# One transposing load for two weights, another order at the head, and a closing loop one tile further ahead

## The chip, the cores and the metric

The kernel runs on one core of a Trainium2 chip. The metric is the device time of one launch in microseconds, shown as the median of several runs. Beside it there is one profiled execution, whose span and trace are read here.

## The reference

Two branches read the same input x (2048 tokens by 512) and are mixed by a gate per token. Branch A is linear attention with a softmax feature map, 32 heads of 16; branch B is a hidden layer of 1376 with ReLU. All inputs and the output are bf16.

```python
g = sigmoid((x * gate_w).sum(-1, keepdims=True))
# branch A
q, k, v = split_heads(x @ wqkv)                       # 32 heads of 16
pq, pk = einsum(q, w_phi), einsum(k, w_phi)           # per head, 16 x 16
phi_q = concat([softmax(pq), softmax(-pq)], -1)       # 32 features
phi_k = concat([softmax(pk), softmax(-pk)], -1)
kv, z = einsum("bhsf,bhsd->bhfd", phi_k, v), phi_k.sum(over s)
o = (phi_q @ kv) / (phi_q @ z + 1e-6)
a = merge_heads(o) @ wo
# branch B
b = relu(x @ w1) @ w2
return g * a + (1 - g) * b
```

## The kernel before

**How an order is written.** The kernel is written out by hand, engine by engine. `p.op(engine, instruction, after=[...], ev=...)` appends one instruction to its engine's list; each engine runs its own list strictly in order, and an instruction waits for the events named in `after`. `p.dma("sp", ...)` does the same for a transfer on SyncE's queue. PSUM has eight banks; `free[bank]` holds the event that releases a bank, set by whatever last evicted it, and the next group of matmuls into that bank waits for it. So what decides when something runs is its place in its engine's list and the bank that it writes.

**The head.** SyncE's queue loads, in this order: half of the first 512 tokens of x (`loadx0`), W1 in row slabs of 128 (`loadw1`, columns 0 to 1023 of each slab; slab 0 in two parts), the other half of the first tokens by a transposing load (`x0t`), slab 3, then columns 1024 to 1375 of all four slabs (`w1r`, line 178), the feature weights, the value weights WV (line 182), the query and the key weights by one transposing load each (`wqk0` and `wqk1`, line 185, 512 x 512), and the other three chunks of x by transposing loads (`x1` to `x3`, line 188). TensorE meanwhile transposes a quarter of x itself, then runs `slab(t)` for t = 0 to 3 (line 520): eight hidden units of the first 512 tokens, each in a bank of its own, one slab of W1 at a time. Two further units follow (`hunit(0, 8)` and `hunit(0, 9)`, line 272).

**The fold.** The feature map is linear up to the softmax, so its weights are folded into the query and key weights: `pre(i)` (line 306) makes one of eight pieces of WQK, 0 to 3 for queries, 4 to 7 for keys, with 4 matmuls of 120 columns each, in banks 0, 1, 6, 7 in turn. A piece is evicted by VectorE (even i, line 311) or ScalarE (odd i, line 313). Before, the order at this place is value tiles 0 and 1, folds 0 to 3, value tile 2, folds 4 to 7, and then `rest(0)` (line 284), the ragged last unit of the hidden layer with the gate's column.

**The passes over 16 tiles of 128 tokens.** In pass m TensorE runs `atile(m)` (line 328, the query and key projections; ScalarE's exponentials of line 348 read them), `kv(m - 3)` (line 426, the running sum over tokens), `vtile(m + 3)` (line 404, the values three tiles ahead, bank 2) and the hidden units that the list `mid[m]` names, each of 4 matmuls of 512 columns. Hidden units take banks 3, 4, 5 in turn (`nextbank`), and so do `rest` and the second of the early value tiles. After the passes come the units in `late`, with the last three `kv` groups between them; `kvfin` on VectorE then turns the sums into KVNZ.

**The closing loop.** For each tile: `nd(m)` (line 458, 8 matmuls, numerator and denominator, banks 0 and 1 or 2 and 3), which VectorE divides (lines 464 and 468) and SyncE transposes into OT by a transfer (line 474); `finB(m)` (line 483, 11 matmuls, the hidden layer's second product) into one of banks 4, 5, 7; `finA(m)` (line 492, 4 matmuls, the attention's output product) into bank 6, which ScalarE scales by the gate into TFA (line 497); and `comb(m)`, VectorE's (1 - g) times finB plus TFA (line 506), which frees finB's bank and is followed by the store (line 511). Before, `finB` runs one tile ahead of `finA`, `nd` three tiles ahead. In pass m it is emitted as

```python
            if m + 1 < NT - 1:
                finB(m + 1, FB[(m + 1) % 3])
```

with `FB = (4, 5, 7)`. `finB` waits for `free[bank]`, and `comb` sets it: `free[bank] = [f"cb{m}{tag}"]`. The last tile is done in two column parts.

Of the kernel before, what the change touches and what calls it, by code (L numbers as in the profile page):

```python
# [68 lines left out]
def bass_gated_mix__linear_kernel_hedgehog__dense_activation_relu__prompt_kernel(  # L69
# [13 lines left out]
    S, D = x2.shape  # L83
    H = A_w_phi.shape[0]
    DH = A_w_phi.shape[1]
    DFF = B_w1.shape[1]
    P = 128
    NT = S // P
    NDT = D // P
# [12 lines left out]
    KU = KT - 1  # L102
    NR = DFF - KU * P

    with ExitStack() as es:
# [55 lines left out]
        def loadw1(t, c0=0, c1=DFF, tag=""):  # L161
            p.dma("sp", lambda e: e.dma_start(  # L162
                out=W1[:, t, c0:c1], in_=B_w1[t * P:(t + 1) * P, c0:c1]), f"w1{t}{tag}", ev=f"w1{t}{tag}")
# [6 lines left out]
        p.early("sp")  # L170
        loadw1(0, 0, 4 * P, "a")
        loadw1(0, 4 * P, 8 * P)
        for t in (1, 2):
            loadw1(t, 0, 8 * P)
        p.dma("sp", lambda e: e.dma_start_transpose(  # L175
            out=XT[:, 2:4, 0:512], in_=x2[0:512, 2 * P:4 * P]), "x0t", ev="x0t")
        loadw1(3, 0, 8 * P)
        p.dma("sp", lambda e: e.dma_start(
            out=W1[:, :, 8 * P:DFF], in_=B_w1[:, 8 * P:DFF].rearrange("(j p) n -> p j n", p=P)), "w1r", ev="w1r")
        p.dma("sp", lambda e: e.dma_start(  # L180
            out=WPS[:, :, :], in_=A_w_phi.rearrange("(g hl) r c -> (hl r) g c", g=NDT)), "wps", ev="wps")
        p.dma("sp", lambda e: e.dma_start(  # L182
            out=WV[:, :, :], in_=A_wqkv[:, 2 * D:3 * D].rearrange("(j p) n -> p j n", p=P)), "wv", ev="wv")
        for i in range(2):
            p.dma("sp", lambda e, i=i: e.dma_start_transpose(  # L185
                out=WQKT[:, 4 * i:4 * i + 4, :], in_=A_wqkv[:, i * D:(i + 1) * D]), f"wqk{i}", ev=f"wqk{i}")
        for c in range(1, NCH):
            p.dma("sp", lambda e, c=c: e.dma_start_transpose(
                out=XT[:, :, c * 512:(c + 1) * 512], in_=x2[c * 512:(c + 1) * 512, :]), f"x{c}", ev=f"x{c}")
# [75 lines left out]
        def nextbank():  # L265
            rot[0] += 1
            return 3 + (rot[0] - 1) % 3
# [32 lines left out]
        def pre(i):  # L300
            which, dt = i // 4, i % 4
            bank = (0, 1, 6, 7)[i % 4]
            dst = WQK[:, which, dt * DE:(dt + 1) * DE]
            after = [f"wqk{which}"] + [f"wbd{g}" for g in range(NDT)] + free[bank]
            for gt in range(NDT):
                p.op("pe", lambda e, gt=gt: e.matmul(  # L306
                    PS[:, bank, gt * 8 * FE:(gt + 1) * 8 * FE], WQKT[:, which * NDT + gt, dt * P:(dt + 1) * P],
                    Wbd[:, gt, :], start=True, stop=True),
                    after=(after if gt == 0 else ()), ev=(f"pm{i}" if gt == NDT - 1 else None))
            if i % 2 == 0:  # L310
                p.op("dve", lambda e: e.tensor_copy(dst, PS[:, bank, 0:DE]), after=[f"pm{i}"], ev=f"pc{i}")
            else:
                p.op("act", lambda e: e.activation(dst, PS[:, bank, 0:DE], ACT.Copy),
                     after=[f"pm{i}"], ev=f"pc{i}")
            free[bank] = [f"pc{i}"]
# [138 lines left out]
        def nd(m):  # L454
            b0 = 2 * (m % 2)
            after = [f"tq{m}", "kvz0"] + free[b0] + free[b0 + 1]
            for g in range(NG):
                p.op("pe", lambda e, g=g: e.matmul(  # L458
                    PS[:, b0 + g // 4, (g % 4) * GW:(g % 4) * GW + 68],
                    PHQ[:, g, m * P:(m + 1) * P], KVNZ[:, g, :], start=True, stop=True),  # L460
                    after=(after if g == 0 else ["kvz1"] if g == 4 else ()), ev=(f"nd{m}" if g == NG - 1 else None))
            r = m % 2
            ob = m % 3
            p.op("dve", lambda e: e.reciprocal(
                RDEN[:, r, :].rearrange("p (g h) -> p g h", g=NG),
                bass.AP(tensor=PS, offset=b0 * 512 + 64, ap=[[EPS, P], [GW, NG], [1, HG]])),
                after=[f"nd{m}"], ev=f"rd{m}")
            p.op("dve", lambda e: e.tensor_tensor(  # L468
                OTM[:, ob, :].rearrange("p (g h d) -> p g h d", g=NG, h=HG),
                bass.AP(tensor=PS, offset=b0 * 512, ap=[[EPS, P], [GW, NG], [DH, HG], [1, DH]]),  # L470
                bass.AP(tensor=RDEN, offset=r * H, ap=[[2 * H, P], [HG, NG], [1, HG], [0, DH]]), ALU.mult),
                after=[f"rd{m}"] + ([f"to{m - 3}"] if m >= 3 else []), ev=f"om{m}")
            free[b0] = free[b0 + 1] = [f"om{m}"]
            p.dma("sp", lambda e: e.dma_start_transpose(
                out=OT[:, :, m * P:(m + 1) * P], in_=OTM[:, ob, :]), f"to{ob}", after=[f"om{m}"], ev=f"to{m}")
# [3 lines left out]
        def finB(m, bank, cs=slice(0, 512), tag=""):  # L479
            n = cs.stop - cs.start  # L480
            for kt in range(KT):
                M = P if kt < KU else NR
                p.op("pe", lambda e, kt=kt, M=M: e.matmul(  # L483
                    PS[:, bank, 0:n], HT[0:M, kt, m * P:(m + 1) * P], W2[0:M, kt, cs],
                    start=(kt == 0), stop=(kt == KT - 1)),
                    after=(["w2", f"hr{m // 4}", f"rl{m // 4}_{KU - 1}"] + free[bank] if kt == 0 else ()),
                    ev=(f"fb{m}{tag}" if kt == KT - 1 else None))
            fbank[(m, tag)] = bank

        def finA(m, bank):  # L490
            for t in range(NDT):
                p.op("pe", lambda e, t=t: e.matmul(  # L492
                    PS[:, bank, :], OT[:, t, m * P:(m + 1) * P], WO[:, t, :],
                    start=(t == 0), stop=(t == NDT - 1)),
                    after=(["wo", f"to{m}"] + free[bank] if t == 0 else ()),
                    ev=(f"fa{m}" if t == NDT - 1 else None))
            p.op("act", lambda e: e.activation(  # L497
                TFA[:, m % 2, :], PS[:, bank, :], ACT.Copy, scale=GT[:, m:m + 1]),
                after=[f"fa{m}", "gt"] + ([f"cb{m - 2}"] if m >= 2 else []), ev=f"ta{m}")
            free[bank] = [f"ta{m}"]  # L500
# [53 lines left out]
        gatecol(0)  # L554
        vtile(0, "dve")
        vtile(1, "act", nextbank())
        for i in range(4):
            pre(i)
        vtile(2, "dve")
        for i in range(4, 8):  # L560
            pre(i)
        rest(0)
        mid = [[(1, 0), (1, 1)], [(1, 2), (1, 3)], [(1, 4), (1, 5)], [(1, 6), (1, 7)], [(1, 8), (1, 9)], [(2, 0)],
               [(1, -1), (2, 1)], [(2, 2), (2, 3)], [(2, 4)], [(2, -1), (2, 5)], [(2, 6), (2, 7)], [(2, 8)],
               [(3, -1), (2, 9)], [(3, 0), (3, 1)], [(3, 2), (3, 3)], []]
        late = [(3, k) for k in range(4, KU)]

        def unit(c, k):
            if k < 0:
                rest(c)  # L570
            else:
                hunit(c, k)

        for m in range(NT):
            atile(m)
            if m >= LAG:
                kv(m - LAG)
            if m + 3 < NT:
                vtile(m + 3)
            for u in mid[m]:  # L580
                unit(*u)
            if m == 3:
                for a, b in ((0, 5), (5, KU)):
                    p.dma("sp", lambda e, a=a, b=b: e.dma_start(
                        out=W2[:, a:b, :], in_=B_w2[a * P:b * P, :].rearrange("(j p) n -> p j n", p=P)),
                        "w2", ev=f"w2{a}")
                p.dma("sp", lambda e: e.dma_start(out=W2[0:NR, KU, :], in_=B_w2[KU * P:DFF, :]), "w2", ev="w2")
            if m == 5:
                for a in range(0, NDT, 2):
                    p.dma("sp", lambda e, a=a: e.dma_start(  # L590
                        out=WO[:, a:a + 2, :], in_=A_wo[a * P:(a + 2) * P, :].rearrange("(j p) n -> p j n", p=P)),
                        "wo", ev="wo" if a else None)
        for i, u in enumerate(late):
            if i == 0:
                kv(NT - 3)
            if i == 2:
                kv(NT - 2)
            if i == 4:
                kv(NT - 1)
                kvfin()  # L600
            unit(*u)
        nd(0)
        qchain(NT - 1)
        gate()
        finB(0, 4)
        nd(1)
        FB = (4, 5, 7)
        for m in range(NT):
            if m > 1 and m + 3 < NT:
                nd(m + 3)  # L610
            if m + 1 < NT - 1:
                finB(m + 1, FB[(m + 1) % 3])
            if m == 1:
                nd(m + 3)
            if m == 0:
                nd(2)
                nd(3)
            finA(m, (6, 2, 0)[max(m - NT + 3, 0)])
            if m < NT - 1:
                comb(m)  # L620
        m = NT - 1
# [40 lines left out]
```

## Time and profile before

| | |
|---|---|
| runs of the kernel before | 147.23 us median of 3 (146.21, 147.23, 147.29) |
| span of the profiled execution | 146.3 us; no other time of that execution is given |
| granted TensorE clock | 1.000 |
| TensorE busy | 143.0 us (98%) |
| VectorE, ScalarE, GpSimd busy | 91.7, 72.4, 52.2 us |
| line 483 (`finB`), 187 matmuls | 40.6 us busy |
| line 272 (hidden units), 128 matmuls | 30.7 us busy |
| line 328 (projections), 128 matmuls | 28.5 us busy |
| transposing weight loads (line 185), 2 | issues of 5.77 and 2.25 us, 8.7 and 5.1 us from issue to landing |

A matmul's busy time in the table includes its passage through the array, which overlaps the next one, so the matmuls' sums exceed the time that they take up: a 128 x 512 matmul is recorded with 0.379 us, and the next one starts 0.216 us after it. Line numbers are those of the listing above. Idle time matters only on the engine that bounds the stage.

### The profile page before, as it was taken

To read this page: it belongs to the slowest core of one execution; us is meant where nothing else is said; L and a number is where in the kernel's file an instruction comes from. 1 tells how busy PE (TensorE), PEld (TensorE's weight loads), DVE (VectorE), ACT (ScalarE), POOL (GpSimd) and SP (SyncE) were. 2 spreads that over 40 slices of the span, in tenths; PEclk is the share of its full clock that TensorE was granted. 3 is DMA by queue.
4 is the path that set the end of the run, shared out by engine and by line. 5 is a ranking of instruction groups with operands and counts; after the bars stand their busy time and mean duration, and the time that the engine had idled before them with its cause. 6 is when DMAs were issued, how large, how long until landed. Compare 5 with 4: busy or idle time off the path is not lost.

```text
span 146.3 us, 2520 instructions
## 1 busy us (share of the span) xinstructions
PE 143.0 (98%) x970; PEld 72.3 (49%) x970; DVE 91.7 (63%) x156; ACT 72.4 (49%) x124; POOL 52.2 (36%) x62
## 2 busy tenths in 40 slices
PE   8999799999999999999999999999999999999994
PEld 3444564444455545544645555554444444444443
DVE  4338627777687878678698977674445555555342
ACT  4134467798778778887878862022221111111150
POOL 2013002778768678688869820300000000000000
DMA  5998998033549984335333431354333223222213
GB/s 150 262 276 163 231 167 186 3 69 72 76 80 328 179 201 73 72 72 108 78 72 75 104 72 31 81 108 117 85 82 78 72 72 76 72 72 74 72 44 106
DMA packets 46517, 16.12 MB, mean 110 GB/s; under 512 B 40392, under 2 KB 46120, under 8 KB 46504
## 3 DMA queue, kind: packets, MB, share of 16 engines
q1 hardware_dynamic: 46352, 15.92, 50.3%
q8 instruction: 8, 0.13, 0.4%
q10 hardware_dynamic: 152, 0.03, 0.1%
q14 instruction: 5, 0.04, 0.1%
HBM read 4.15 MB, written 2.10 MB: 43 GB/s over the span
## 4 chain that ended last, share of the span: by engine, by line
PE 86%; SPq 7%; DMA 4%; DVE 1%; issue 0%
PE PS L483 26%; PE PS L328 18%; PE PS L272 18%; PE PS L492 9%; PE PS L404 8%; SPq L185 4%; DMA PHQ<-in_A_wqkv_dram 4%; PE PS L458 3%; PE PS L426 3%; PE PS L284 2%; SPq L162 2%; SPq L175 1%; PE PS L306 1%; DVE WQK L506 1%; SPq L182 0%
## 5 line engine op out<-in xcount | busy, mean ns | idle before, releaser
L483 PE MATMUL PS<-W,HT 128*128 128x512 bf16 (+4 forms) x187 | 40.6, 366 | 0.0
L372 POOL TENSOR_TENSOR EB<-EB,SC 128x1024 bf16<-128x1024 bf16 x15 | 28.9, 1930 | 23.4 <-DVE SC L370 23.4
L348 ACT ACTIVATE EB<-PS 128x480 bf16<-128x480 f32 (+1 forms) x44 | 30.1, 756 | 14.2 <-PE PS L328 14.2
L497 ACT ACTIVATE TFA<-PS,GT 128x512 bf16<-128x512 f32 x16 | 11.0, 687 | 42.7 <-PE PS L492 36.6
L272 PE MATMUL PS<-XT,W 128*128 128x512 bf16 x128 | 30.7, 379 | 0.0
L328 PE MATMUL PS<-WQK,XT 128*128 128x480 bf16 x128 | 28.5, 366 | 0.0
L368 DVE TENSOR_REDUCE ZB<-EB 128x64 f32<-128x1024 bf16 x15 | 18.3, 1220 | 14.7 <-ACT EB L348 14.7
L506 DVE SCALAR_TENSOR_TENSOR WQK<-PS,OMG,TFA 128x512 bf16<-128x512 f32 (+2 forms) x17 | 12.2, 719 | 23.6 <-ACT TFA L497 22.4
L483 PEld LDWEIGHTS PS<-W,HT 128*128 128x128 bf16 (+1 forms) x187 | 17.0, 98 | 17.4
L258 ACT ACTIVATE HT<-PS 128x512 bf16<-128x512 f32 x35 | 20.3, 614 | 7.4 <-PE PS L520 5.6
L328 PEld LDWEIGHTS PS<-WQK,XT 128*128 128x128 bf16 x128 | 12.5, 98 | 13.6
L383 DVE TENSOR_REDUCE ZB<-EB 128x64 f32<-128x1024 bf16 x16 | 18.6, 1164 | 0.0
L272 PEld LDWEIGHTS PS<-XT,W 128*128 128x128 bf16 x128 | 12.0, 98 | 13.2
L392 POOL TENSOR_TENSOR EB<-EB,SC 128x512 bf16<-128x512 bf16 x16 | 16.9, 1059 | 1.3
L404 PE MATMUL PS<-WV,XT 128*128 128x512 bf16 x64 | 16.2, 378 | 0.0
L492 PE MATMUL PS<-WO,OT 128*128 128x512 bf16 x64 | 16.1, 378 | 0.0
L468 DVE TENSOR_TENSOR WQK<-PS,RDEN 128x512 bf16<-128x512 f32 x16 | 11.1, 692 | 0.5
L492 PEld LDWEIGHTS PS<-WO,OT 128*128 128x128 bf16 x64 | 6.1, 97 | 7.2
L414 ACT ACTIVATE VS<-PS 128x512 bf16<-128x512 f32 x14 | 8.5, 608 | 2.0 <-PE PS L404 2.0
L370 DVE RECIPROCAL SC<-ZB 128x64 f32<-128x64 f32 x16 | 8.8, 553 | 0.5
L458 PEld LDWEIGHTS PS<-KVNZ,PHQ 128*128 128x128 bf16 x128 | 6.1, 97 | 3.6
L404 PEld LDWEIGHTS PS<-WV,XT 128*128 128x128 bf16 x64 | 5.4, 97 | 4.8
(57 smaller groups left out, 85.7 us busy)
## 6 DMA issues: line engine op xcount, KB each, us to landing
out_dram<-WQK SPq DMA_DIRECT2D x15, 128.0 KB, 1.7
W<-in_B_w_dram SPq DMA_DIRECT2D x2, 640.0 KB, 5.8
W<-in_B_w_dram SPq DMA_DIRECT2D x3, 256.0 KB, 3.8
WV<-in_A_wqkv_dram SPq DMA_DIRECT2D x1, 512.0 KB, 6.5
WO<-in_A_wo_dram SPq DMA_DIRECT2D x2, 256.0 KB, 3.0
W<-in_B_w_dram SPq DMA_DIRECT2D x1, 352.0 KB, 5.1
OT<-in_A_x_dram SPq DMA_DIRECT2D x2, 128.0 KB, 2.3
W<-in_B_w_dram SPq DMA_DIRECT2D x2, 128.0 KB, 3.0
```

Source lines behind the costliest of these rows:

```text
L258: p.op("act", lambda e: e.activation(dst, src, ACT.Relu), after=[f"h{c}_{kt}"], ev=ev)
L272: p.op("pe", lambda e, t=t: e.matmul(PS[:, bank, :], W1[:, t, kt * P:(kt + 1) * P], XT[:, t, c * 512:(c + 1) * 512], start=(t == 0), stop= ...
L328: p.op("pe", lambda e, dt=dt, which=which: e.matmul(PS[:, which, 0:DE], XT[:, dt, m * P:(m + 1) * P], WQK[:, which, dt * DE:(dt + 1) * DE] ...
L348: p.op("act", lambda e: e.activation(dst, s_, ACT.Exp, scale=scale), after=[f"qk{m}"] + busy, ev=ev)
L368: p.op("dve", lambda e: e.tensor_reduce(zk, ek, AX.X, ALU.add), after=[emk, f"cst{b}"], ev=f"zk{m}")
L372: p.op("pool" if m < NT - 1 else "dve", lambda e: e.tensor_tensor(EB[:, b, 3, :].rearrange("p (g f) -> p g f", f=DH), EB[:, b, 2, :].rearr ...
L383: p.op("dve", lambda e: e.tensor_reduce(ZB[:, b, 0:64].rearrange("p (h s) -> p h s", s=2), bass.AP(tensor=EB, offset=base, ap=[[EBS, P], [ ...
L392: p.op("pool", lambda e: e.tensor_tensor(EB[:, b, 0, :].rearrange("p (h s f) -> p h s f", h=H, s=2)[:, :, 1, :], EB[:, b, 1, :].rearrange( ...
L404: p.op("pe", lambda e, dt=dt: e.matmul(PS[:, bank, :], XT[:, dt, m * P:(m + 1) * P], WV[:, dt, :], start=(dt == 0), stop=(dt == NDT - 1)), ...
L483: p.op("pe", lambda e, kt=kt, M=M: e.matmul(PS[:, bank, 0:n], HT[0:M, kt, m * P:(m + 1) * P], W2[0:M, kt, cs], start=(kt == 0), stop=(kt = ...
L492: p.op("pe", lambda e, t=t: e.matmul(PS[:, bank, :], OT[:, t, m * P:(m + 1) * P], WO[:, t, :], start=(t == 0), stop=(t == NDT - 1)), after ...
L506: p.op("dve", lambda e: e.scalar_tensor_tensor(out=OSB[:, ob, cs], in0=PS[:, bank, 0:n], scalar=OMG[:, m:m + 1], in1=TFA[:, m % 2, cs], op ...
```

## The change

At the head, slabs 2 and 3 of W1 are loaded as whole rows of 1376 columns, and the load of the remaining columns covers slabs 0 and 1 only. The query and key weights come in one transposing load of 512 x 1024 with one event, `wqk`, for which all eight folds wait. Value tiles 0 to 3 stand ahead of all the folds, value tile 3 in a bank of `nextbank`, evicted by ScalarE; the passes no longer make value tile 3, and pass 0 has three hidden units in place of two, with everything behind shifted by one, so that `late` has five units and not six. In the closing loop, `finB(0)` stands ahead of `nd(0)`, `finB(1)` ahead of `nd(1)`, and pass m runs `finB(m + 2)` and no longer `finB(m + 1)`, in the same three banks; `finA` of the last three tiles takes banks 2, 0 and 6.

```diff
         loadw1(0, 4 * P, 8 * P)
-        for t in (1, 2):
-            loadw1(t, 0, 8 * P)
+        loadw1(1, 0, 8 * P)
+        loadw1(2)
         p.dma("sp", lambda e: e.dma_start_transpose(
             out=XT[:, 2:4, 0:512], in_=x2[0:512, 2 * P:4 * P]), "x0t", ev="x0t")
-        loadw1(3, 0, 8 * P)
+        loadw1(3)
         p.dma("sp", lambda e: e.dma_start(
-            out=W1[:, :, 8 * P:DFF], in_=B_w1[:, 8 * P:DFF].rearrange("(j p) n -> p j n", p=P)), "w1r", ev="w1r")
+            out=W1[:, 0:2, 8 * P:DFF], in_=B_w1[0:2 * P, 8 * P:DFF].rearrange("(j p) n -> p j n", p=P)),
+            "w1r", ev="w1r")
...
-        for i in range(2):
-            p.dma("sp", lambda e, i=i: e.dma_start_transpose(
-                out=WQKT[:, 4 * i:4 * i + 4, :], in_=A_wqkv[:, i * D:(i + 1) * D]), f"wqk{i}", ev=f"wqk{i}")
+        p.dma("sp", lambda e: e.dma_start_transpose(out=WQKT[:, :, :], in_=A_wqkv[:, 0:2 * D]), "wqk", ev="wqk")
...
-            after = [f"wqk{which}"] + [f"wbd{g}" for g in range(NDT)] + free[bank]
+            after = ["wqk"] + [f"wbd{g}" for g in range(NDT)] + free[bank]
...
         vtile(0, "dve")
         vtile(1, "act", nextbank())
-        for i in range(4):
-            pre(i)
         vtile(2, "dve")
-        for i in range(4, 8):
+        vtile(3, "act", nextbank())
+        for i in range(8):
             pre(i)
         rest(0)
-        mid = [[(1, 0), (1, 1)], [(1, 2), (1, 3)], [(1, 4), (1, 5)], ...
+        mid = [[(1, 0), (1, 1), (1, 2)], [(1, 3), (1, 4)], [(1, 5), (1, 6)], ...
...
-        late = [(3, k) for k in range(4, KU)]
+        late = [(3, k) for k in range(5, KU)]
...
-            if m + 3 < NT:
+            if 0 < m and m + 3 < NT:
                 vtile(m + 3)
...
+        FB = (4, 5, 7)
+        finB(0, FB[0])
         nd(0)
         qchain(NT - 1)
         gate()
-        finB(0, 4)
+        finB(1, FB[1])
         nd(1)
-        FB = (4, 5, 7)
         for m in range(NT):
             if m > 1 and m + 3 < NT:
                 nd(m + 3)
-            if m + 1 < NT - 1:
-                finB(m + 1, FB[(m + 1) % 3])
+            if m + 2 < NT - 1:
+                finB(m + 2, FB[(m + 2) % 3])
             if m == 1:
                 nd(m + 3)
             if m == 0:
                 nd(2)
                 nd(3)
-            finA(m, (6, 2, 0)[max(m - NT + 3, 0)])
+            finA(m, (6, 2, 0, 6)[max(m - NT + 4, 0)])
             if m < NT - 1:
                 comb(m)
```

More of the change, by code (lines that the diff above doesn't have):

```diff
@@ L556, in bass_gated_mix__linear_kernel_hedgehog__dense_activation_relu__prompt_kernel @@
         vtile(1, "act", nextbank())
-        for i in range(4):
-            pre(i)
         vtile(2, "dve")
-        for i in range(4, 8):
+        vtile(3, "act", nextbank())
+        for i in range(8):
             pre(i)
         rest(0)
-        mid = [[(1, 0), (1, 1)], [(1, 2), (1, 3)], [(1, 4), (1, 5)], [(1, 6), (1, 7)], [(1, 8), (1, 9)], [(2, 0)],
-               [(1, -1), (2, 1)], [(2, 2), (2, 3)], [(2, 4)], [(2, -1), (2, 5)], [(2, 6), (2, 7)], [(2, 8)],
-               [(3, -1), (2, 9)], [(3, 0), (3, 1)], [(3, 2), (3, 3)], []]
-        late = [(3, k) for k in range(4, KU)]
+        mid = [[(1, 0), (1, 1), (1, 2)], [(1, 3), (1, 4)], [(1, 5), (1, 6)], [(1, 7), (1, 8)], [(1, 9), (2, 0)], [(2, 1)],
+               [(1, -1), (2, 2)], [(2, 3), (2, 4)], [(2, 5)], [(2, -1), (2, 6)], [(2, 7), (2, 8)], [(2, 9)],
+               [(3, -1), (3, 0)], [(3, 1), (3, 2)], [(3, 3), (3, 4)], []]
+        late = [(3, k) for k in range(5, KU)]
         def unit(c, k):
```

## The prediction

> **What bounds the kernel now.** I first read the page's busy shares: TensorE is busy for 143.0 of 146.3 us. I then read the chain that ended last, to see whether anything else stands in it. After 17.57 us there is nothing on it but matmul groups, laid end to end, until the last two evictions.
>
> ```profile
> span 146.3 us, 2520 instructions
> PE 143.0 (98%) x970; PEld 72.3 (49%) x970; DVE 91.7 (63%) x156; ACT 72.4 (49%) x124; POOL 52.2 (36%) x62
> ```
>
> ```profile
> 12.41 5.12 DMA PHQ<-in_A_wqkv_dram
> 17.53 0.04 issue
> 17.57 1.01 PE PS L306 x16
> 18.59 0.69 PE PS L284 x16
> 19.28 1.62 PE PS L328 x8
> ...
> 101.99 0.25 PE PS L458 x8
> 102.25 2.38 PE PS L483 x11
> 104.62 0.86 PE PS L492 x4
> 105.49 0.26 PE PS L458 x8
> ```
>
> The columns are start, length, what. The last lines are one pass of the closing loop, 0.25 + 2.38 + 0.86 = 3.49 us. The reader should see that there is no gap: whatever wait the change adds on TensorE lengthens the time one for one, and whatever it saves must come from TensorE's idle time, all of it ahead of 17.57 us. TensorE's own timeline around the weight transposes shows how little that is:
>
> ```profile
> 12.89 1.89 PE L404 MATMUL PS<-WV,XT 128*128 128x512 bf16 x8
> 15.30 1.01 PE L306 MATMUL PS<-Wbd,PHQ 128*128 128x120 bf16 x16 [0.52 <-DMA PHQ<-in_A_wqkv_dram]
> 16.15 1.03 PE L404 MATMUL PS<-WV,XT 128*128 128x512 bf16 x4
> 17.57 1.01 PE L306 MATMUL PS<-Wbd,PHQ 128*128 128x120 bf16 x16 [0.40 <-DMA PHQ<-in_A_wqkv_dram]
> ```
>
> Below I count in starts of matmuls: a 128x512 one takes its slot of 0.216 us and ends 0.379 us after its start. The two idle stretches are then 14.62 to 15.30 and 17.01 to 17.57, 1.24 us together.
>
> **The head: loads.** The bytes stay the same. Slabs 2 and 3 carry 96 KB more each, the rest load 180 KB less. By landings, the 256 KB of slab 2 came 0.77 us after the slab before (340 GB/s), and the 360 KB rest load, in rows of 704 bytes, 1.98 us after slab 3 (182 GB/s). So 180 KB cost 0.99 us in short rows and 0.53 in long ones: up to 0.46 us saved, at least 0. I take 0.45, because slab 2's row is the nearest for whole rows. Price on the way: the first chunk's transposing load (issued at 3.03, 4.4 us to landing, so 7.48) comes behind 96 KB more, 0.28 us later, 7.76. Slab 2's first matmul stood at 7.68, so TensorE waits about 0.13 us. That costs nothing while it still waits for the query and key weights later; without this cover it costs 0.13. The values' weights land at 12.5 now, ahead of their use at 12.89, so bringing them forward gains nothing.
>
> **The head: one transposing load.** The two loads land 2.71 and 2.28 us after what precedes them (12.54, 15.25, 17.53). No row shows one of 512x1024. Nearest are the loads of 512x512: three more of them land 1.92, 3.19 and 1.76 us apart. Two halves therefore cost 3.5 to 6.4 us. I take the sum of the very rows that are replaced, 4.99 us. With 0.45 us off ahead of it the load lands at 17.1, between 15.6 and 18.9, and TensorE starts the folds at F = 17.13. A page of the Trainium skill says that one large transfer is the better one: "DMA: Bandwidth & Descriptors", section "Latency and other measured facts", gives 261 GB/s for a transposing load, whereas these two moved 1 MB in 4.99 us, 210 GB/s. By that figure the load would take 4.0 us, TensorE would come first, and the head would gain 0.7 us instead of what follows; the rows decide here.
>
> **The head: order.** Value tiles 2 and 3 run from 14.68 (tile 2 waits for tile 0's eviction of the same bank, 13.95 + 0.69) to 16.41, 0.13 us later with the stall above: TensorE is idle until F. Then eight folds go through four banks. A fold is 0.21 us of matmuls, and its eviction is slower: VectorE starts the first 0.42 us after the folds' start (15.72 against 15.30) and one takes 0.66, so the fifth fold waits for its bank until F + 1.11 where TensorE is through with four at F + 0.85 (0.26 lost); the seventh likewise until F + 1.68 (0.15 lost). The folds end at F + 2.1, the ragged unit (0.69) at F + 2.8. There the attention projections start; now they start at 19.12, which is 1.55 after 17.57. One value tile (4 x 0.216 = 0.86) has moved from behind this point to ahead of it; the unit that takes its place in pass 0 is missing at the end, so the passes keep their length and 0.86 comes off. Sum of the head: (17.13 + 2.8) - 19.12 - 0.86 = **-0.05 us**. Bounds: with F = 16.54, where TensorE itself is the limit, -0.6; with F = 18.9, +1.7.
>
> **The tail: who frees a bank.** The diff also moves the hidden layer's second product (the 11 matmuls of line 483, finB) one tile further ahead: in pass m it is now tile m + 2, in the same three banks 4, 5, 7. Tile m + 2 takes the bank of tile m - 1, which is freed by comb(m - 1), and that waits for ScalarE's eviction of finA(m - 1), the four matmuls just ahead on TensorE. Before, it was the bank of tile m - 2, freed a whole pass earlier. The timeline of one pass prices this chain:
>
> ```profile
> 100.97 1.03 PE L492 MATMUL PS<-WO,OT 128*128 128x512 bf16 x4
> 101.83 0.42 PE L458 MATMUL PS<-KVNZ,PHQ 128*128 128x68 bf16 x8
> 102.03 0.69 ACT L497 ACTIVATE TFA<-PS,GT 128x512 bf16<-128x512 f32 x1 [2.81 <-PE PS L492]
> 102.75 0.75 DVE L506 SCALAR_TENSOR_TENSOR WQK<-PS,OMG,TFA 128x512 bf16<-128x512 f32 x1 [1.76 <-ACT TFA L497]
> 103.42 0.35 DVE L464 RECIPROCAL RDEN<-PS 128x32 f32<-128x32 f32 x1
> 103.53 0.34 SPq L511 DMA_DIRECT2D out_dram<-WQK  x1
> ```
>
> finA's slots end at 101.83. ScalarE starts at 102.03, VectorE's combination at 102.75 and ends at 103.50; SyncE's store, which waits for the same event, goes at 103.53. TensorE would go at 103.54, that is 1.70 us after finA, and has only the eight matmuls of line 458 (0.25 us) to fill it: **1.45 us idle in every pass** from m = 2 to 12, 11 x 1.45 = 15.95. Behind the waiting matmul stand finB's other ten, the next finA and everything after it on TensorE; ScalarE and VectorE have nothing else to do there. VectorE's order keeps comb(m - 1) ahead of the next division (line 464), so this chain isn't longer.
>
> Pass m = 1 has no line 458 group ahead of finB(3). Its comb(0) stands on VectorE behind two divisions and products (tiles 2 and 3). From finA(0)'s end: the last of these products is done about 1.1 us later, comb(0) 0.74 after that, so TensorE waits **1.87 us**.
>
> The start of the tail: finB(0) now comes ahead of nd(0), on bank 4. One more value tile takes a bank of the rotation 3, 4, 5, and the last hidden unit (the 38th in turn, before the 37th) lands in bank 4, not in bank 3. finB(0) therefore waits for that unit's ReLU on ScalarE:
>
> ```profile
> 87.99 0.50 PEld L458 LDWEIGHTS PS<-KVNZ,PHQ 128*128 128x128 bf16 x8
> 88.20 0.42 PE L458 MATMUL PS<-KVNZ,PHQ 128*128 128x68 bf16 x8
> 88.40 0.60 ACT L258 ACTIVATE HT<-PS 128x512 bf16<-128x512 f32 x1 [0.27 <-PE PS L272]
> ```
>
> The unit's slots end at 88.20, the ReLU at 89.00, so TensorE starts at 89.03: **0.83 us**. The wait that finB(0) was put there to cover is smaller: with one unit fewer behind the last kv group, VectorE's kvfin, which now ends 0.6 us before it is needed, would be 0.3 us late. nd(0)'s transposing store lands in 2.7 us, under finB(1) and finB(2), and costs nothing. At the end finA(12) to finA(15) run together; bank 6 is free again 0.9 us after finA(12), under two others (1.73): nothing.
>
> **Sum.** -0.05 + 0.83 + 1.87 + 15.95 = +18.6 us. The page's span of 146.3 becomes 164.9. The page gives no time beside the span; the span lies within the runs (146.21 to 147.29) and 0.9 below their median of 147.23, and 147.2 + 18.6 = **165.8 us**. A restart of TensorE after a wait isn't shown for these shapes: after the wait at 15.30 the first slot is 0.01 us longer, and the longest slot at any start is 0.43 us, at 4.19, 0.21 over the later ones. Over 13 waits that is 0.1 to 2.7 us; I take the lower end, since it stands after a wait at full pace.
>
> **Rivals.**
> 1. **The clock falls as well.** At the start the same 128x512 matmuls are 0.427 us apart, then 0.216: TensorE has a slow pace, and 29% idle in each pass of 4.94 us might bring it back. The work of twelve passes would double: 12 x 3.49 = 41.9, 207.7 us. Against it: between 14.62 and 17.57 TensorE was idle for 1.24 of 2.95 us, 42%, and the value tile at 16.15 still went at 0.216. The skill speaks for it: "TensorE: Matmul & The Clock Gate", section "A second HAM failure mode: psum-queue depth-cycling", has small idle gaps between groups of banks make the clock swing. Section "Part 1: The HAM clock gate" of the same page asks for an idle window of some 3.4 us. By the first rule the time would be up to this rival's, by the second that of the forecast. 5%.
> 2. **The ring holds, not slower.** If comb(m - 1) were done by the time finB(m + 2) has its turn, the tail would keep 3.49 us a pass and only the head, with the 0.83, would count: 147.2 - 0.05 + 0.83 = 148.0, no slower than a measurement can tell; with the load at its early bound and no wait on the ReLU, 146.6. It decides only where the chain finA to comb takes under 0.25 us; it takes 1.70. 3%, for an error in my reading of the order.
> 3. **The chain is longer.** If division and product (0.39 + 0.61) came ahead of each comb on VectorE, 11 us more: 177 us. The order written out speaks against it. 3%.
>
> **How the numbers follow.** The forecast has 89%. Its range: from the fastest run, 146.2 + 18.6 - 0.6 for the early load and less some tenths if a chain of two hand-overs is a little shorter, 163.5; upward 147.3 + 18.6 + 1.7 and some of the restarts, 168.5. That holds 8 in 10; rivals 1 to 3 lie outside. A measurement of this kernel can tell about 1% from no change. Faster by over 1% 0.02, within 1% 0.02, slower 0.96.
>
> **What would show it.** In the changed profile: TensorE's share about 87%; waits of line 483's matmuls on VectorE's combination, some twelve, together near 17.8 us, and one on the ReLU near 0.8; the passes 4.94 us apart; ScalarE's line 497 and VectorE's line 506 on the chain that ended last; the projections' first matmul near 19.9. Passes of 3.49 us would refute the tail, spacings of 0.427 in them would be rival 1, a fold start far from 17.1 the load's price.

## The result and the profile after

The changed kernel takes 166.5 us (median of four runs, 166.42 to 166.67) against 147.24 us before (146.21 to 147.29): ratio 1.1346, 95% interval 1.1304 to 1.1389. The forecast was 165.8 us, 163.5 to 168.5. The profiled execution has a span of 165.1 us and a time of 166.42 us, and its granted clock is 1.000.

The page of the kernel after, its span and its busy shares:

```profile
span 165.1 us, 2505 instructions
PE 145.2 (88%) x970; PEld 72.7 (44%) x970; DVE 91.7 (56%) x156; ACT 72.4 (44%) x124; POOL 52.1 (32%) x62
```

TensorE has the same 970 matmuls; its share fell from 98% to 88%. VectorE and ScalarE do what they did, 91.7 and 72.4 us. So nothing became slower, something waits. The waits of the kernel after (engine, line of the waiting instruction, who released it: total us, how often, the longest):

```profile
PE PS L482 <- DVE WQK L505: 16.4, 12, 1.7
PE PS L482 <- ACT HT L257: 0.8, 1, 0.8
```

Line 482 is now `finB`'s matmul, line 505 the combination that frees its bank, line 257 the ReLU. Before, no matmul of `finB` waited for anything. A wait begins in this view when the last matmul ahead is through the array, about 0.16 us after its slot, so the slots lost are a little more: counted from the matmuls' starts, 0.94 us for the ReLU, 1.87 us for the first combination, and 1.47 to 1.57 us for each of the other eleven, 16.5 us together. That makes 19.3 us, and the tail's whole account. (The 0.16 us, 13 times, are also nearly all of the 2.2 us by which TensorE's busy time rose, from 143.0 to 145.2 us: a passage through the array that no next matmul covers.) The chain that ended last shows how a pass looks (start, length, what):

```profile
107.27 0.88 PE PS L491 x4
108.15 0.03 issue
108.17 0.70 ACT TFA L496
108.87 0.03 issue
108.89 0.76 DVE WQK L505
109.66 0.05 issue
109.70 2.55 PE PS L482 x11
112.25 0.88 PE PS L491 x4
```

Before, these were matmul groups and nothing else. Now the chain leaves TensorE in every pass: `finA`, ScalarE's eviction, VectorE's combination, and only then the next `finB`. A pass has gone from 3.49 to 4.98 us, and to 5.07 in three of the eleven.

### The profile page after: what moved, and what is told of

Same layout as the page of the kernel before. It is cut to its first block, busy times and chain, and to the rows that moved or that the text cites. A ratio compares the mean times of both kernels' runs of the same rounds, so it can differ in the third digit from the quotient of the medians.

```text
span 165.1 us, 2505 instructions
## 1 busy us (share of the span) xinstructions
PE 145.2 (88%) x970; PEld 72.7 (44%) x970; DVE 91.7 (56%) x156; ACT 72.4 (44%) x124; POOL 52.1 (32%) x62
## 4 chain that ended last, share of the span: by engine, by line
PE 81%; DVE 7%; ACT 5%; DMA 3%; issue 2%; SPq 1%
PE PS L482 24%; PE PS L271 17%; PE PS L327 16%; PE PS L403 8%; PE PS L491 8%; DVE WQK L505 6%; ACT TFA L496 5%; DMA XT<-in_A_x_dram 3%; PE PS L425 2%; PE PS L519 2%; PE PS L283 2%; SPq L162 1%; PE PS L305 1%; PE PS L457 1%; DVE WQK L467 0%
## 5 line engine op out<-in xcount | busy, mean ns | idle before, releaser
L463 DVE RECIPROCAL RDEN<-PS 128x32 f32<-128x32 f32 x16 | 5.6, 350 | 7.6 <-PE PS L457 7.6
```

## The experiments

Each experiment ran on one chip beside the kernel before; ratios are to that. Spans are of the profiled execution; the time of an execution is 1.2 to 1.4 us above its span in the runs below. The diffs show the lines that matter for the argument; lines left out are marked by `...` or belong to the same edit.

### Each half alone

The head of the change with the old closing loop:

```diff
 # the changed kernel with
+        nd(0)
+        qchain(NT - 1)
+        gate()
+        finB(0, 4)
+        nd(1)
...
+            if m + 1 < NT - 1:
+                finB(m + 1, FB[(m + 1) % 3])
```

> The head of the changed kernel with the closing loop of the kernel before (finB one tile ahead, finB(0) behind nd(0)). Bank theory (the loss is the wait of finB(m + 2) for the bank that comb(m - 1) frees): the passes of the closing loop come back to 3.49 us. The head brings 0.62 us forward, as in the changed kernel; nd(0) then waits about 0.27 us for kvfin and finB(0) about 0.42 us more for the ReLU in bank 4, so the span is 146.3 - 0.62 + 0.69 = 146.4 us and the time 147.3 us, the same as before. Head theory (the other order at the head costs the time by later buffers or a slower clock): it stays near 165 us.

Measured: 147.95 us, ratio 1.0076 (1.0046 to 1.0106), span 146.8 us. The passes are back at 3.49 us, so the head theory is out. The head isn't neutral, though: it costs some 1.1 us. Of this 0.19 and 0.48 us are the two waits of `nd(0)` and `finB(0)`, for which 0.27 and 0.42 had been expected. The rest is at the head; see below.

The closing loop alone, on the kernel before:

```diff
 # the kernel before with
+        FB = (4, 5, 7)
+        finB(0, FB[0])
         nd(0)
...
+            if m + 2 < NT - 1:
+                finB(m + 2, FB[(m + 2) % 3])
```

> The kernel before with the closing loop of the changed one alone. Bank theory: no wait for the ReLU, since the last hidden unit lies in bank 3; one wait of 1.88 us in pass 1 and eleven of 1.50 us, 18.4 in all: span 164.7 us, time 165.8 us, passes of 4.98 us. Head theory: passes of 3.49 us, about 147 us. Clock theory (the gaps bring a slow pace of TensorE back): matmuls of 512 columns 0.43 us apart in the passes; bank theory: 0.216 us.

Measured: 165.3 us, ratio 1.1257 (1.1222 to 1.1291), span 164.0 us; that is 18.5 us over the kernel before beside it, where 18.4 had been expected. One pass in its timeline:

```profile
110.97 1.03 PE L492 MATMUL PS<-WO,OT 128*128 128x512 bf16 x4
111.84 0.42 PE L458 MATMUL PS<-KVNZ,PHQ 128*128 128x68 bf16 x8
112.04 0.69 ACT L497 ACTIVATE TFA<-PS,GT 128x512 bf16<-128x512 f32 x1 [4.29 <-PE PS L492]
112.76 0.75 DVE L506 SCALAR_TENSOR_TENSOR WQK<-PS,OMG,TFA 128x512 bf16<-128x512 f32 x1 [3.24 <-ACT TFA L497]
113.57 0.60 PE L483 MATMUL PS<-W,HT 128*128 128x512 bf16 x2 [1.31 <-DVE WQK L506]
```

The same two engines, with the same durations as in the kernel before (0.69 and 0.75 us), now stand between two matmul groups. Nothing of the new head is in this kernel; the closing loop alone carries the loss. It has no wait for the ReLU.

### Banks or distance

Two tiles ahead and three banks came together. These two kernels take them apart. First, still two tiles ahead, with a fourth bank:

```diff
 # the changed kernel with
-            b0 = 2 * (m % 2)
+            b0 = 0
...
-        FB = (4, 5, 7)
+        FB = (4, 5, 7, 2)
...
-                finB(m + 2, FB[(m + 2) % 3])
+                finB(m + 2, FB[(m + 2) % 4])
```

> The changed kernel, finB still two tiles ahead, but in four banks (4, 5, 7, 2); nd has banks 0 and 1 alone in return. Bank theory: finB(m + 2) takes the bank that comb(m - 2) freed a pass earlier, so its waits go and the passes last 3.49 us. New wait: nd(3) right behind nd(2) waits for the same banks, 1.3 us, once. From 165.1: 11 x 1.49 and 0.56 net in passes 0 and 1 go, span 148.1 us, time 149.3 us. If two tiles ahead costs in itself (VectorE's or SyncE's order, the stores, the clock), the passes stay near 4.98 us and the time near 166 us.

Measured: 150.92 us, ratio 1.0277 (1.0248 to 1.0306), span 149.4 us. The passes, from the chain that ended last:

```profile
101.80 0.02 issue
101.82 0.37 DVE RDEN L463
102.19 0.02 issue
102.21 0.70 DVE WQK L467
102.92 0.14 issue
103.05 0.41 PE PS L457 x8
103.47 2.38 PE PS L482 x11
105.84 0.87 PE PS L491 x4
106.71 0.25 PE PS L457 x8
106.96 2.38 PE PS L482 x11
```

From 103 us on TensorE has no gap and a pass lasts 3.49 us: running two tiles ahead costs nothing once the bank is there. The span is 1.3 us above what was expected, and the trace shows where: `nd`, left with one pair of banks, waits for the product of the tile before it twice, not once (1.43 us, and the 0.57 us that the first lines above end). At the end VectorE's combination of the last tile then waits about 1 us for a store, because four combinations fall close together and share three output buffers:

```profile
146.91 0.88 DVE L505 SCALAR_TENSOR_TENSOR WQK<-PS,OMG,TFA 128x384 bf16<-128x384 f32 x2 [1.95 <-DMA out_dram<-WQK]
```

Then the opposite: one tile ahead as it always was, with two banks in place of three.

```diff
 # the kernel before with
-        FB = (4, 5, 7)
+        FB = (4, 5)
...
-                finB(m + 1, FB[(m + 1) % 3])
+                finB(m + 1, FB[(m + 1) % 2])
```

> The kernel before, finB one tile ahead as it was, but in two banks (4, 5) in place of three; the last tile's first part takes bank 5. Bank theory: finB(m + 1) now needs the bank of finB(m - 1), the very wait of the changed kernel, without any of its other edits: 1.84 us in pass 1, 1.50 us in passes 2 to 12, 1.75 us in pass 13, 20.1 us in all; span 166.4 us, time 167.4 us. If the loss comes from running two tiles ahead, the time stays at 147.2 us.

Measured: 167.25 us, ratio 1.1389 (1.1362 to 1.1416), span 166.1 us; its waits:

```profile
PE PS L483 <- DVE WQK L506: 18.0, 13, 1.7
```

This kernel has none of the change's edits and loses as much. What decides is the number of banks less the distance: it was two (three banks, one ahead), and at one, as in the changed kernel (three banks, two ahead) and here (two banks, one ahead), the bank comes back only through the `finA` that has just gone.

### What fills the wait

```diff
 # the changed kernel with
-            if m > 1 and m + 3 < NT:
-                nd(m + 3)
             if m + 2 < NT - 1:
                 finB(m + 2, FB[(m + 2) % 3])
-            if m == 1:
+            if m >= 1 and m + 3 < NT:
                 nd(m + 3)
```

> The changed kernel with nd(m + 3) behind finB(m + 2) in every pass, so that nothing stands between finA(m - 1) and the matmuls that wait for its bank. Bank theory: the end of the wait is fixed by finA, ScalarE and VectorE, so the 0.25 us of nd come on top in eleven passes: passes of 5.23 us, waits of 1.73 us, span 165.1 + 2.8 = 167.9 us, time 169.2 us. If something else sets the passes (the stores, SyncE's queue), they stay at 4.98 us.

Measured in one execution: 170.5 us, span 169.2 us. The waits in the passes are 1.73 us (1.82 in three of them) where they were 1.48, and the passes 5.24 us. The 0.25 us of `nd` did hide that much of the chain. The span is 1.3 us more than expected, since `nd(15)` is now late for `finA(13)` and `finA(15)` at the end, which wait 0.57 and 0.62 us:

```profile
PE PS L491 <- DMA OT<-WQK: 0.5, 1, 0.5
PE PS L491 <- DVE WQK L467: 0.4, 1, 0.4
```

### The loads and the head

The first profile of before had 1.24 us of idle TensorE at the head. It was run again, unchanged.

> The kernel before once more, for its loads. If the first profile caught a late one: value weights near 11.3 us, the two halves of the query and key weights near 14.2 and 16.4 us, no idle TensorE between value tiles and folds, the fold of the keys begun 1.7 us after that of the queries. If the loads are always that late: 12.5, 15.3 and 17.5 us and 1.24 us of idle TensorE again.

Measured: 146.45 us, span 145.2 us. TensorE's timeline around the folds:

```profile
13.01 1.89 PE L404 MATMUL PS<-WV,XT 128*128 128x512 bf16 x8
14.73 1.00 PE L306 MATMUL PS<-Wbd,PHQ 128*128 128x120 bf16 x16
15.57 1.03 PE L404 MATMUL PS<-WV,XT 128*128 128x512 bf16 x4
16.43 1.00 PE L306 MATMUL PS<-Wbd,PHQ 128*128 128x120 bf16 x16
17.27 0.86 PE L284 MATMUL PS<-W,XT 128*128 128x97 bf16 x16
```

There is no wait left in it: the loads landed at 11.32, 13.89 and 16.08 us (12.54, 15.25 and 17.53 in the first profile). The two kernels with the old loads, `tail_alone` and `two_banks`, agree: 14.39 and 16.62, 13.89 and 16.21, and no wait either. The first profile had caught a late one; in the other three of these four executions the head of before had nothing to give. The head of the changed kernel, at the same place:

```profile
12.99 3.71 PE L403 MATMUL PS<-WV,XT 128*128 128x512 bf16 x16
16.54 2.28 PE L305 MATMUL PS<-Wbd,PHQ 128*128 128x120 bf16 x32
18.66 0.86 PE L283 MATMUL PS<-W,XT 128*128 128x97 bf16 x16
```

The 32 fold matmuls take 2.1 us from first start to the next group, where before two groups of 16 took 0.84 us each. In between they wait 0.29 and 0.13 us for the evictions of their four banks, and value tile 2 waits 0.09 us; together 0.51 us.

The loads alone, on the kernel before:

```diff
 # the kernel before with
+        loadw1(2)
...
+        loadw1(3)
...
+        p.dma("sp", lambda e: e.dma_start_transpose(out=WQKT[:, :, :], in_=A_wqkv[:, 0:2 * D]), "wqk", ev="wqk")
```

> The kernel before with the changed kernel's loads alone (whole rows of W1's slabs 2 and 3, one transposing load of the query and key weights); value tiles, folds, passes and closing loop as before. One-load theory (the one load lands some 0.9 us earlier than the second of two, but 1.2 us later than the first): the folds of the queries, ready at 14.7 to 15.3 us, wait until 15.4 to 15.6, up to 0.7 us; those of the keys no longer depend on a load; slab 2 waits up to 0.35 us for the first chunk of x, which comes 96 KB later. 0.5 us over the kernel before, ratio 1.003. If the loads gain as the first profile had it, 0.4 us less: 0.997.

Measured: 147.16 us, ratio 1.0024 (1.0006 to 1.0043). In the profiled execution the one load landed at 15.57 us and the first fold waited 0.31 us for it; slab 2 waited 0.11 us for x. The loads gain nothing here, because the first fold needs only the first half.

Then the head of the change without the two waits that it brought to the closing loop (`nd(0)` for kvfin, `finB(0)` for the ReLU):

```diff
 # the new loads and head, the passes and closing loop of before, with
-            finB(0, 4)
+            finB(0, 5)
...
-        FB = (4, 5, 7)
+        FB = (5, 7, 4)
```

> The loads and the order at the head of the changed kernel; passes, late units and closing loop of the kernel before, finB's banks turned to (5, 7, 4) so that finB(0) needs no ReLU of the last unit. Fold theory (the eight folds in four banks wait for their evictions, some 0.5 us, and the kernel before loses nothing at this place in most of its executions): 0.5 us over the kernel before, ratio 1.0035, no wait in the closing loop. Load theory, as the profile of before had it (TensorE waits 1.24 us for the weights, the new head does not): 0.6 us less than before, ratio 0.996.

Measured: 147.91 us, ratio 1.0087 (1.0064 to 1.0110). The folds' 0.42 us and value tile 2's 0.09 are there, and a wait that was not expected: pass 0, short of its value tile, is over so soon that the projections of tile 1 wait 0.36 us. That is 0.87 us of the 1.28 that the ratio stands for. In the profiled execution the rest lies ahead of slab 2, whose first matmul stands at 8.18 us, against 7.80 in `before_again`. The unchanged head has it anywhere from 7.68 to 8.42 us in its four profiles, so this part can't be put down to the change.

```diff
 # head_tuned with
-            bank = (0, 1, 6, 7)[i % 4]
+            bank = (0, 1, 6, 7, 5, 4, 2, 3)[i]
...
-        rest(0)
+        rest(0, 6)
```

> As head_tuned, with the eight folds in eight different banks (0, 1, 6, 7, 5, 4, 2, 3) and the ragged unit in bank 6. Fold theory: no wait between folds, 0.5 us less than head_tuned, ratio to before about 1.000; where an execution of before has late loads, a little below. Load theory: 1.1 us less than before, ratio 0.993.

Measured: 147.07 us, ratio 1.0027 (1.0012 to 1.0043), a little over the 1.000 that was expected. The 32 fold matmuls go without a wait; 0.36 us in pass 0 and 0.09 in value tile 2 remain, and slab 2 waits 0.32 us for the late chunk of x.

At last, the merged load and the new order with W1's loads as before, the folds in eight banks, three units in pass 0, and the closing loop one tile ahead:

```diff
 # the changed kernel with the edit of folds_eight_banks and
-        loadw1(2)
+        loadw1(2, 0, 8 * P)
...
-        loadw1(3)
+        loadw1(3, 0, 8 * P)
...
+            if m + 1 < NT - 1:
+                finB(m + 1, FB[(m + 1) % 3])
```

> The changed kernel's one transposing load, its four value tiles ahead of the folds and its passes, without the waits found so far: W1's loads as in the kernel before, the folds in eight banks, the ragged unit in bank 6, finB one tile ahead in banks 5, 7, 4. Sum of the waits that are left: 0.09 us in value tile 2, 0.2 us of nd(0) for kvfin. Theory: nothing else in the new order costs or gains, since the kernel before has no idle TensorE at the head in most executions: ratio 1.002. If the new order gains in itself, below 0.997; if it costs in itself, as in folds_eight_banks, 1.003 and more.

Measured: 146.78 us against 146.77, ratio 1.0010 (0.9989 to 1.0031). The profiled execution has three short waits left, 0.09 us in value tile 2, 0.19 of `nd(0)` for kvfin and 0.27 of slab 2. So the new order has neither gain nor cost that this measurement tells from nothing, some 0.3 us. No version ran faster than the kernel before beyond its interval.

## Why the prediction was right, and where its terms were off

**The tail: right in mechanism, place and size.** The step "who frees a bank" gave 1.45 us in eleven passes and 1.87 us in pass 1; they measured 1.47 to 1.57 and 1.87. `two_banks` makes the same waits without the change, `four_banks` takes them away with it, and `no_cover` lengthens them by just the 0.25 us that was said to fill them. The ReLU's wait was 0.94 and not 0.83 us. The term that is too small in both is the restart of TensorE: between the end of VectorE's instruction and the first matmul lay 0.05 us in most passes and 0.14 in three, while 0.03 had been taken over from SyncE's queue. (After the ReLU it was 0.14 as well.)

**The load: the duration was off by a fifth.** The step "one transposing load" took 4.99 us, the sum of the two that are replaced. One load took 4.06 us after the value weights (11.37 to 15.43 us), and 3.8 to 4.4 in the other runs with it; pairs took 4.8 to 5.2. The figure of the Trainium skill that the prediction weighed against the rows, 261 GB/s from "DMA: Bandwidth & Descriptors", section "Latency and other measured facts", was the better one: 1 MB in 4.06 us is 258 GB/s. (The page gives it for a non-contiguous middle dimension, and 350 to 400 GB/s otherwise; no run here shows which of the two this load is.) So the folds started at 16.54 us, TensorE's own limit, which was the early end of the range, and not at 17.13. The waits of the folds behind that were foretold well: 0.26 and 0.15 us, measured 0.29 and 0.13.

**A cost whose cover went.** Slab 2's wait for the first chunk of x was put at 0.13 us, hidden under a later wait for the weights. With the weights early there was no later wait: it measured 0.34 us in the profile after (7.79, where slab 1 began at 5.72 and takes 1.73) and nothing hid it. (In that execution slab 1 happened to begin 0.35 us earlier than in `before_again`, 5.72 against 6.07, which makes up for it in the comparison below.) The wait hangs on when slab 1 begins: it was 0.35 us in `four_banks` and nothing in `no_cover`, with the same loads. The 96 KB behind the estimate are 88, since the issues of slabs 2 and 3 went from 256 to 344 KB; that changes it by 0.02 us.

**W1's whole rows: no gain shown.** 0.45 us had been expected from them. The value weights behind them landed at 11.37 us, and at 11.2 to 11.4 in `before_again`, `tail_alone` and `two_banks`, which have the old loads. The gain had been measured against a late execution.

**The head's sum.** -0.05 us was foretold, -0.62 measured against the first profile (the last hidden unit ends at 87.58, not 88.20), and this hides the step that failed: that profile stood for before. Against `before_again`, 87.06, the head costs 0.52 us. More firmly: from slab 2's first matmul to the end of the last hidden unit it is 79.26 us in each of `before_again`, `tail_alone` and `two_banks`, and 79.79 us in each of `after`, `head_alone`, `four_banks` and `no_cover`, which have the new head and its passes: 0.53 us more. The tail's 19.3 us and this 0.5 are, within 0.1, the 19.9 us between the spans 145.2 and 165.1.

**The total: luck in part.** The span came out at 165.1 us where 164.9 had been summed up, but two errors cancel in it: the tail was 0.7 us dearer than foretold, the head 0.6 cheaper against a profile that was itself late. The time was 166.5 and not 165.8 us mostly for another reason. The forecast set 147.2 us beside the span of 146.3, only 0.9 more, while the executions with both figures have 1.2 to 1.4 more; that is 0.3 to 0.5 of the 0.7 us.

**The rivals.** The clock didn't fall: the granted clock is 1.000 and 128x512 matmuls in the passes are 0.216 us apart, with TensorE idle for 13.8 of the 51 us between 99 and 150. The swinging clock of the section "A second HAM failure mode: psum-queue depth-cycling" of "TensorE: Matmul & The Clock Gate" did not show with these gaps; the other, "Part 1: The HAM clock gate", with its idle window of some 3.4 us, agrees with gaps of 1.5 us that change nothing. The ring did not hold (rival 2): the bank came 1.5 us after `finB`'s turn. The chain was not longer (rival 3): no division stood in it from pass 2 on.

## What to carry to other kernels

For a ring of buffers, write down who frees the buffer that the next producer takes, and count what the producer's own queue holds between that release's cause and its use: when the distance grows by one and the ring has no buffer to spare, the ring must grow by one, or the release falls onto the critical path, less the work that still stands between. A step "further ahead" buys nothing where the engine has no idle time, and what one profile shows as idle has to be seen in a second execution before it is counted as gain. Merging the two loads shortened the pair here and delayed its first half, so it fits only an order that needs both at once.

## What the runs showed of the hardware

- The loads at the head vary between executions of one and the same kernel: the value weights landed at 12.54 and at 11.32 us, and the spans were 146.3 and 145.2 us.
- TensorE's slow pace at the start ends at different times. Until then matmuls of 512 columns are 0.38 to 0.43 us apart, afterwards 0.216. The first matmul of all starts at 0.38 or 0.39 us in each of the twelve profiles, yet in `after` none of slab 0's matmuls, from 3.76 us on, was slow, while in `two_banks` the slow pace lasted until 6.25 us. "TensorE: Matmul & The Clock Gate", "Part 1: The HAM clock gate", has this move by 0.5 us either way; here it moved by more. Together with waits for loads this sets when slab 1 begins, between 5.6 and 6.7 us.
- From the end of a VectorE instruction to the matmul that waits for it the chain shows either 0.05 or 0.14 us, in the same loop. In `after`, `tail_alone`, `two_banks` and `no_cover` alike, the 0.14 stands ahead of tiles 4, 8 and 12 of `finB` alone. There its first matmul also names the events of a new group of 512 tokens (`hr{m // 4}`) in its `after`; that this is the reason is not shown.
